# Squeeze-and-excitation on one core: keeping 20 more rows per partition on chip, 18 of them in PSUM, and a one-column gate computation

## The chip, the cores and the metric

The kernel runs on one core of a Trainium2 chip. The metric is the device time of one execution in microseconds (us), lower is better. A "row" in this text is one pixel's 384 channels in bf16, 768 bytes. Each of the 128 partitions owns 512 rows, so one row per partition is 98,304 bytes. The profile calls TensorE (matmuls) PE, its weight loads PEld, VectorE DVE, ScalarE ACT and SyncE SP. SBUF and PSUM are the core's two on-chip memories, HBM is the memory outside it, and DMA is the transfers between them.

## The reference

```python
# x: (1, 256, 256, 384), w_down: (384, 24), w_up: (24, 384), all bf16
def reference(x, w_down, w_up):
    s = x.mean(axis=(1, 2))                    # one mean per channel over 65,536 pixels
    s = sigmoid(silu(s @ w_down) @ w_up)       # a gate per channel
    return x * s[:, None, None, :]
```

Every input value must be read before the first output value is known. The input (50.33 MB) does not fit on chip, so part of it has to be read twice.

## The kernel before

In the load pass the input streams into SBUF, tile after tile of 16 rows, and TensorE sums each row over the partitions with a column of ones as weights. The last tiles that fit stay resident. Then a short chain of small operations makes the gate. In the second pass DVE multiplies the resident tiles in place and they are stored; as a slot's store lands, one of the tiles that did not stay is loaded into it again ("reload").

```python
    # 16 slots of 16 rows and one of 15: 271 of 512 rows stay, 241 are reloaded
    n_full = min(avail // (R * ROW_BYTES), rows_pp // R)
    extra_rows = (avail - n_full * R * ROW_BYTES) // ROW_BYTES
    slot_rows = [R] * n_full + ([extra_rows] if extra_rows else [])
    # ... cut: the reload tiles come first in the load pass, the resident ones last
    p1_last_split = [4, 2]      # last tile loaded in 4 pieces, the one before in 2
    # ... cut: for each tile: nc.sync.dma_start(...), then accumulate_rows:
            nc.tensor.matmul(sum_ps[:, :], lhsT=ones_bf[:, 0:1],
                             rhs=xt_ap[:, r * C : (r + 1) * C], ...)

    # the chain between the passes; KC = 3 blocks of P = 128 channels
    nc.scalar.activation(mean_sb[:], sum_ps[:], ACT.Copy, scale=1.0 / float(NROWS))
    for k in range(KC):         # channels onto partitions, repeated in 128 columns
        nc.tensor.matmul(psT[:, k * P : (k + 1) * P],
                         lhsT=mean_sb[0:1, k * P : (k + 1) * P],
                         rhs=ones_row[0:1, 0:P], start=True, stop=True)
    nc.vector.tensor_copy(sT_b[:], psT[:])
    for k in range(KC):
        nc.tensor.matmul(z_ps[:, :], lhsT=wd_bf[:, k, :],
                         rhs=sT_b[:, k * P : (k + 1) * P], ...)
    nc.scalar.activation(sig_sb[:], z_ps[:], ACT.Sigmoid)
    nc.vector.tensor_mul(silu_sb[:], z_ps[:], sig_sb[:])
    nc.tensor.matmul(z2_ps[:, :], lhsT=silu_sb[:, :], rhs=wu_bf[:, :], ...)
    nc.scalar.activation(s_bc[:], z2_ps[:], ACT.Sigmoid)     # 128 equal rows of the gate

    # second pass, per piece: multiply on DVE, store from ACT's queue
            nc.vector.tensor_tensor(out=x3, in0=x3,
                in1=s_bc[:, None, :].to_broadcast([P, rp, C]), op=ALU.mult)
            nc.scalar.dma_start(out=dst[...], in_=xs_)
    # ... cut: after a resident tile's store, a reload into its slot from SP's queue
```

Of the kernel before, what the change touches and what calls it, by code (L numbers as in the profile page):

```python
# [8 lines left out]
FP32 = mybir.dt.float32  # L9
BF16 = mybir.dt.bfloat16  # L10
ACT = mybir.ActivationFunctionType
ALU = mybir.AluOpType


@with_exitstack
def kernel(
# [7 lines left out]
    nc = tc.nc  # L24
    P = nc.NUM_PARTITIONS

    B, H, W, C = x.shape
    Cr = w_down.shape[1]
# [3 lines left out]
    KC = C // P  # L32
# [4 lines left out]
    esize = mybir.dt.size(x.dtype)  # L37
    ROW_BYTES = C * esize
    rows_pp = NROWS // P

    R = 16
    budget = 212_352
    misc_bytes = 4224
    first_split = [3, 2, 2]
    first_chunks = [2, 6, 8]
    p1_last_split = [4, 2]

    avail = budget - misc_bytes
    while R > 1 and rows_pp % R != 0:
        R //= 2  # L50
    n_full = min(avail // (R * ROW_BYTES), rows_pp // R)
    extra_rows = (avail - n_full * R * ROW_BYTES) // ROW_BYTES
    extra_rows = min(extra_rows, R - 1, rows_pp - n_full * R)
    if extra_rows < 1:
        extra_rows = 0
    slot_rows = [R] * n_full + ([extra_rows] if extra_rows else [])
    S = len(slot_rows)
    assert S >= 1
    res_rows = sum(slot_rows)
    assert res_rows <= rows_pp  # L60
    reload_rows = rows_pp - res_rows
    reload_tiles = [R] * (reload_rows // R)
# [3 lines left out]
    tiles = []  # L66
    row = 0
    rr_slot = 0
    for nr in reload_tiles:
        if nr < R and extra_rows and nr <= extra_rows:  # L70
            v = n_full
        else:
            v = rr_slot % n_full
            rr_slot += 1
        tiles.append(dict(row=row, nrows=nr, resident=False, slot=v))
        row += nr
    for v in range(S):
        nr = slot_rows[v]
        tiles.append(dict(row=row, nrows=nr, resident=True, slot=v))
        row += nr  # L80
    assert row == rows_pp

# [1 line left out]
    opp = of.rearrange("(p r) c -> p (r c)", p=P)  # L84

    consts = ctx.enter_context(tc.tile_pool(name="consts", bufs=1))
    small = ctx.enter_context(tc.tile_pool(name="small", bufs=1))
    slots_pool = ctx.enter_context(tc.tile_pool(name="slots", bufs=1))
    psum = ctx.enter_context(tc.tile_pool(name="psum", bufs=1, space=bass.MemoryType.PSUM))

    ones_bf = consts.tile([P, 1], BF16)
    nc.vector.memset(ones_bf[:], 1.0)  # L92
    ones_row = consts.tile([1, P], BF16)
# [11 lines left out]
    slots = [  # L105
        slots_pool.tile([P, slot_rows[v] * C], BF16, tag=f"slot{v}", name=f"slot{v}")
        for v in range(S)
    ]

    sum_ps = psum.tile([1, C], FP32)  # L110
    total_mm = rows_pp
    mm_state = {"i": 0}

    def accumulate_rows(xt_ap, nrows):
        for r in range(nrows):
            i = mm_state["i"]
            nc.tensor.matmul(  # L117
                sum_ps[:, :],
                lhsT=ones_bf[:, 0:1],
                rhs=xt_ap[:, r * C : (r + 1) * C],  # L120
                start=(i == 0),
                stop=(i == total_mm - 1),
            )
            mm_state["i"] = i + 1

    for k, t in enumerate(tiles):
        nr = t["nrows"]
        xt = slots[t["slot"]][:, 0 : nr * C]
        nparts = 1
        from_end = len(tiles) - 1 - k  # L130
        if from_end < len(p1_last_split):
            nparts = max(1, min(p1_last_split[from_end], nr))
        base = nr // nparts
        rem_r = nr - base * nparts
        r0 = 0
        for q in range(nparts):
            rp = base + (1 if q < rem_r else 0)
            if rp == 0:
                continue
            nc.sync.dma_start(  # L140
                out=xt[:, r0 * C : (r0 + rp) * C],
                in_=xpp[:, (t["row"] + r0) * C : (t["row"] + r0 + rp) * C],
            )
            accumulate_rows(xt[:, r0 * C : (r0 + rp) * C], rp)
            r0 += rp
    assert mm_state["i"] == total_mm

    mean_sb = small.tile([1, C], BF16)
    nc.scalar.activation(mean_sb[:], sum_ps[:], ACT.Copy, scale=1.0 / float(NROWS))  # L149
    psT = psum.tile([P, KC * P], FP32)  # L150
    for k in range(KC):
        nc.tensor.matmul(  # L152
            psT[:, k * P : (k + 1) * P],
            lhsT=mean_sb[0:1, k * P : (k + 1) * P],
            rhs=ones_row[0:1, 0:P],
            start=True,
            stop=True,
        )
    sT_b = small.tile([P, KC * P], BF16)
    nc.vector.tensor_copy(sT_b[:], psT[:])  # L160
    z_ps = psum.tile([Cr, P], FP32)
    for k in range(KC):
        nc.tensor.matmul(  # L163
            z_ps[:, :],
            lhsT=wd_bf[:, k, :],
            rhs=sT_b[:, k * P : (k + 1) * P],
            start=(k == 0),
            stop=(k == KC - 1),
        )
    sig_sb = small.tile([Cr, P], BF16)  # L170
    nc.scalar.activation(sig_sb[:], z_ps[:], ACT.Sigmoid)  # L171
    silu_sb = small.tile([Cr, P], BF16)
    nc.vector.tensor_mul(silu_sb[:], z_ps[:], sig_sb[:])  # L173
    z2_ps = psum.tile([P, C], FP32)
    nc.tensor.matmul(  # L175
        z2_ps[:, :], lhsT=silu_sb[:, :], rhs=wu_bf[:, :], start=True, stop=True
    )
    s_bc = small.tile([P, C], BF16)
    nc.scalar.activation(s_bc[:], z2_ps[:], ACT.Sigmoid)  # L179

    def scale_and_store(xt, nrows, dst, parts=1):
        if isinstance(parts, (list, tuple)):
            chunks = list(parts)
            rest = nrows - sum(chunks)
            assert rest >= 0
            if rest:
                chunks.append(rest)
        else:
            parts = max(1, min(parts, nrows))
            base = nrows // parts  # L190
            extra = nrows - base * parts
            chunks = [base + (1 if q < extra else 0) for q in range(parts)]
        r0 = 0
        for rp in chunks:
            if rp == 0:
                continue
            xs_ = xt[:, r0 * C : (r0 + rp) * C]
            x3 = xs_.rearrange("p (r c) -> p r c", c=C)
            nc.vector.tensor_tensor(  # L199
                out=x3,  # L200
                in0=x3,
                in1=s_bc[:, None, :].to_broadcast([P, rp, C]),
                op=ALU.mult,
            )
            nc.scalar.dma_start(out=dst[:, r0 * C : (r0 + rp) * C], in_=xs_)  # L205
            r0 += rp

    resident = [t for t in tiles if t["resident"]]
    reload = [t for t in tiles if not t["resident"]]
    queue = [(t, t["slot"]) for t in resident]  # L210
    pending_reload = list(reload)
    qi = 0
    while qi < len(queue):
        t, v = queue[qi]
        qi += 1
        parts = 1
        if qi - 1 < len(first_split):
            parts = first_split[qi - 1]
        if qi == 1 and first_chunks and sum(first_chunks) <= t["nrows"]:
            parts = first_chunks  # L220
        nr = t["nrows"]
        xt = slots[v][:, 0 : nr * C]
        scale_and_store(
            xt, nr, opp[:, t["row"] * C : (t["row"] + nr) * C], parts=parts
        )
        for pi, rt in enumerate(pending_reload):
            if rt["nrows"] <= slot_rows[v]:
                pending_reload.pop(pi)
                xr = slots[v][:, 0 : rt["nrows"] * C]
                nc.sync.dma_start(  # L230
                    out=xr,
                    in_=xpp[:, rt["row"] * C : (rt["row"] + rt["nrows"]) * C],
                )
                queue.append((rt, v))
                break
    assert not pending_reload, pending_reload


# [28 lines left out]
```

## Time and profile before

| | before |
|---|---|
| median of the first 6 runs | 308.13 us (307.71 to 310.08) |
| span of the profiled run | 306.4 us |
| HBM read and written | 74.06 and 50.33 MB |
| DVE, PE busy | 35%, 30% |
| last reduction matmul to first scaling | 123.86 to 127.29 us |

From the page of the kernel before: the DMA rows of the 40 slices of the span (busy tenths, then GB/s), and the bytes.

```profile
DMA  8999999999999998199999999999999999999996
GB/s 301 424 427 422 422 433 422 422 425 425 428 421 425 428 419 338 40 360 397 431 430 425 430 430 435 423 430 431 436 425 428 430 428 427 431 430 433 427 430 279
HBM read 74.06 MB, written 50.33 MB: 406 GB/s over the span
```

Everywhere but at both ends and around one slice in the middle, the transfers run at 421 to 436 GB/s. The table of stretches of the same kernel says it more exactly (the columns are the stretch and its length, the busy us and the count of PE, PEld, DVE, ACT and POOL, then the granted clock, the DMA share and GB/s): the load pass, the second pass with loads and stores mixed, and its end with stores alone.

```profile
20.00:114.00 94.00, 69.25 (x403) 33.60 (x402) 0.00 (x0) 0.00 (x0) 0.00 (x0) 1.00 1.01 425
137.00:250.00 113.00, 0.00 (x0) 0.00 (x0) 92.23 (x29) 0.00 (x0) 0.00 (x0) 0.50 1.01 427
254.00:300.00 46.00, 0.00 (x0) 0.00 (x0) 0.36 (x1) 0.00 (x0) 0.00 (x0) 0.50 1.01 430
```

DVE and PE wait for the transfers, so outside the gap a faster engine is worth nothing here. Only two things are: fewer bytes, and less time in which nothing moves. The timeline of the kernel before around the gap (start and duration in us, engine, operation, and in brackets how long the engine had been idle and what ended that):

```profile
115.83 8.02 PE L117 MATMUL sum_ps<-slot,ones_bf 128*1 128x384 bf16 x47 [0.94 <-DMA slot<-in_x_dram]
123.88 0.48 ACT L149 ACTIVATE mean_sb<-sum_ps 1x384 bf16<-1x384 f32 x1 [120.40 <-PE sum_ps L117]
124.41 0.34 PE L152 MATMUL psT<-ones_row,mean_sb 1*128 1x128 bf16 x3 [0.57 <-ACT mean_sb L149]
124.79 0.56 DVE L160 CAST sT_b<-psT 128x384 bf16<-128x384 f32 x1 [123.76 <-PE psT L152]
125.40 0.33 PE L163 MATMUL z_ps<-sT_b,wd_bf 128*24 128x128 bf16 x3 [0.65 <-DVE sT_b L160]
125.76 0.27 ACT L171 ACTIVATE sig_sb<-z_ps 24x128 bf16<-24x128 f32 x1 [1.40 <-PE z_ps L163]
126.06 0.28 DVE L173 TENSOR_TENSOR silu_sb<-z_ps,sig_sb 24x128 bf16<-24x128 f32 x1 [0.72 <-ACT sig_sb L171]
126.40 0.33 PE L175 MATMUL z_ps<-wu_bf,silu_sb 24*128 24x384 bf16 x1 [0.67 <-DVE silu_sb L173]
126.77 0.49 ACT L179 ACTIVATE s_bc<-z_ps 128x384 bf16<-128x384 f32 x1 [0.74 <-PE z_ps L175]
127.29 13.44 DVE L199 TENSOR_TENSOR slot<-slot,s_bc 128x768 bf16<-128x768 bf16 x8 [0.95 <-ACT s_bc L179]
```

Read the starts from top to bottom: each step begins when the one above ends, so the 3.43 us from 123.86 to 127.29 are one serial chain, and nothing is stored before it is over. Two more readings, from the groups of instructions by shape and from the list of waits of the kernel before:

```profile
L199 DVE TENSOR_TENSOR slot<-slot,s_bc 128x6144 bf16<-128x6144 bf16 x28 | 92.2, 3355 | 21.1 <-DMA slot<-in_x_dram 21.1
L199 DVE TENSOR_TENSOR slot<-slot,s_bc 128x3072 bf16<-128x3072 bf16 x5 | 8.4, 1751 | 0.0
DVE slot L199 <- DMA slot<-in_x_dram: 21.7, 7, 4.0
```

A multiply costs 0.52 ns per column ((3355 - 1751) / 3072) plus about 0.15 us, and DVE stands idle for 21.7 us waiting for reloads.

### The profile page before, as it was taken

The numbers are of one execution on the slowest core, as the hardware profiler recorded it, in microseconds if no ns is written. First come the engines' busy times: TensorE is split into PE (matmuls) and PEld (weight loads), VectorE is DVE, ScalarE is ACT, GpSimd is POOL, SyncE is SP. The second block draws the span as 40 slices with busy tenths as digits, with TensorE's granted clock in tenths as the row PEclk, the third lists the DMA queues.
The fourth block names the chain that finished last, engine by engine and source line by source line (L and its number), as shares of the span: only waits on it lengthen the run. The fifth ranks groups of instructions, "written<-read, shape, count | busy, mean of one in ns | idle before, by whom it ended". The sixth has DMA issues, their size and how long they took to land.

```text
span 306.4 us, 1330 instructions
## 1 busy us (share of the span) xinstructions
PE 90.4 (30%) x519; PEld 43.6 (14%) x519; DVE 106.7 (35%) x42; ACT 2.7 (1%) x5; POOL 0.2 (0%) x4
## 2 busy tenths in 40 slices
PE   0877577777777778200000000000000000000000
PEld 0433233333333334100000000000000000000000
DVE  0000000000000000499999999998444441000000
ACT  1000000000000000100000000000000000000000
POOL 0000000000000000000000000000000000000000
PEclk9999999999999999955555555555555555555555
DMA  8999999999999998199999999999999999999996
GB/s 301 424 427 422 422 433 422 422 425 425 428 421 425 428 419 338 40 360 397 431 430 425 430 430 435 423 430 431 436 425 428 430 428 427 431 430 433 427 430 279
DMA packets 13403, 124.49 MB, mean 406 GB/s; under 512 B 1852, under 2 KB 2388, under 8 KB 3924
## 3 DMA queue, kind: packets, MB, share of 16 engines
q1 hardware_dynamic: 7632, 74.03, 57.6%
q10 hardware_dynamic: 5764, 50.37, 39.1%
q8 instruction: 4, 0.07, 0.1%
q14 instruction: 3, 0.02, 0.0%
HBM read 74.06 MB, written 50.33 MB: 406 GB/s over the span
## 4 chain that ended last, share of the span: by engine, by line
DMA 74%; DVE 5%; PE 3%; ACT 0%; issue 0%; SPq 0%; ACTq 0%; DVEq 0%
DMA slot<-in_x_dram 36%; DMA out_dram<-slot 33%; DMA wd_bf<-in_w_down_dram 5%; DVE slot L199 5%; PE sum_ps L117 3%; DVE sT_b L160 0%; ACT s_bc L179 0%; ACT mean_sb L149 0%; PE psT L152 0%; PE z_ps L175 0%; PE z_ps L163 0%; DVE silu_sb L173 0%; ACT sig_sb L171 0%; ACTq L205 0%; DVEq L199 0%
## 5 line engine op out<-in xcount | busy, mean ns | idle before, releaser
L199 DVE TENSOR_TENSOR slot<-slot,s_bc 128x6144 bf16<-128x6144 bf16 (+5 forms) x37 | 105.7, 2922 | 22.7 <-DMA slot<-in_x_dram 21.7
L117 PE MATMUL sum_ps<-slot,ones_bf 128*1 128x384 bf16 x512 | 89.4, 329 | 34.4 <-DMA slot<-in_x_dram 34.4
L117 PEld LDWEIGHTS <-ones_bf 128*1 128x1 bf16 x512 | 43.1, 84 | 80.3 <-issue 42.2
L160 DVE CAST sT_b<-psT 128x384 bf16<-128x384 f32 x1 | 0.6, 558 | 123.8 <-PE psT L152 123.8
L149 ACT ACTIVATE mean_sb<-sum_ps 1x384 bf16<-1x384 f32 x1 | 0.5, 481 | 120.4 <-PE sum_ps L117 120.4
L103 ACT ACT_TABLE_LOAD x1 | 1.3, 1283 | 2.0 <-issue 2.0
L175 PE MATMUL z_ps<-wu_bf,silu_sb 24*128 24x384 bf16 x1 | 0.3, 332 | 0.7 <-DVE silu_sb L173 0.7
L173 DVE TENSOR_TENSOR silu_sb<-z_ps,sig_sb 24x128 bf16<-24x128 f32 x1 | 0.3, 279 | 0.7 <-ACT sig_sb L171 0.7
L163 PE MATMUL z_ps<-sT_b,wd_bf 128*24 128x128 bf16 x3 | 0.3, 217 | 0.6 <-DVE sT_b L160 0.6
L152 PE MATMUL psT<-ones_row,mean_sb 1*128 1x128 bf16 x3 | 0.3, 217 | 0.6 <-ACT mean_sb L149 0.6
L179 ACT ACTIVATE s_bc<-z_ps 128x384 bf16<-128x384 f32 x1 | 0.5, 491 | 0.7 <-PE z_ps L175 0.7
L163 PEld LDWEIGHTS <-wd_bf 128*24 128x24 bf16 x3 | 0.2, 90 | 0.7 <-issue 0.6
L92 DVE MEMSET ones_bf<- 128x1 bf16 x1 | 0.1, 59 | 0.8 <-PEq L251 0.8
L152 PEld LDWEIGHTS <-mean_sb 1*128 1x128 bf16 x3 | 0.2, 92 | 1.0 <-ACT mean_sb L149 1.0
L171 ACT ACTIVATE sig_sb<-z_ps 24x128 bf16<-24x128 f32 x1 | 0.3, 267 | 1.4 <-PE z_ps L163 1.4
L175 PEld LDWEIGHTS <-silu_sb 24*128 24x128 bf16 x1 | 0.1, 91 | 0.8 <-DVE silu_sb L173 0.8
L103 ACT ACTIVATE warm<-warm 1x8 bf16<-1x8 bf16 x1 | 0.2, 208 | 0.0
L94 DVE MEMSET ones_row<- 1x128 bf16 x1 | 0.2, 165 | 0.0
L251 POOL MEMSET const-uint8-127<- 128x1 uint8 x1 | 0.1, 102 | 0.0
L251 POOL MEMSET const-bfloat16-1.0<- 128x1 bf16 x1 | 0.1, 101 | 0.0
L251 POOL MEMSET const-float32-0.0<- 128x1 f32 x1 | 0.1, 98 | 0.2 <-issue 0.2
L251 POOL MEMSET const-float32-1.0<- 128x1 f32 x1 | 0.1, 98 | 0.0
(1 smaller groups left out, 0.1 us busy)
## 6 DMA issues: line engine op xcount, KB each, us to landing
slot<-in_x_dram SPq DMA_DIRECT2D x45, 1536.0 KB, 19.1
out_dram<-slot ACTq DMA_DIRECT2D x28, 1536.0 KB, 29.1
out_dram<-slot ACTq DMA_DIRECT2D x5, 768.0 KB, 8.4
slot<-in_x_dram SPq DMA_DIRECT2D x2, 768.0 KB, 27.7
out_dram<-slot ACTq DMA_DIRECT2D x1, 1440.0 KB
slot<-in_x_dram SPq DMA_DIRECT2D x3, 384.0 KB, 20.5
out_dram<-slot ACTq DMA_DIRECT2D x1, 576.0 KB, 2.8
slot<-in_x_dram SPq DMA_DIRECT2D x1, 288.0 KB, 14.7
```

What stands on the lines that cost most here:

```text
L103: nc.scalar.activation(warm[:], warm[:], ACT.Sigmoid)
L117: nc.tensor.matmul(sum_ps[:, :], lhsT=ones_bf[:, 0:1], rhs=xt_ap[:, r * C : (r + 1) * C], start=(i == 0), stop=(i == total_mm - 1),)
L149: nc.scalar.activation(mean_sb[:], sum_ps[:], ACT.Copy, scale=1.0 / float(NROWS))
L152: nc.tensor.matmul(psT[:, k * P : (k + 1) * P], lhsT=mean_sb[0:1, k * P : (k + 1) * P], rhs=ones_row[0:1, 0:P], start=True, stop=True,)
L160: nc.vector.tensor_copy(sT_b[:], psT[:])
L163: nc.tensor.matmul(z_ps[:, :], lhsT=wd_bf[:, k, :], rhs=sT_b[:, k * P : (k + 1) * P], start=(k == 0), stop=(k == KC - 1),)
L171: nc.scalar.activation(sig_sb[:], z_ps[:], ACT.Sigmoid)
L173: nc.vector.tensor_mul(silu_sb[:], z_ps[:], sig_sb[:])
L175: nc.tensor.matmul(z2_ps[:, :], lhsT=silu_sb[:, :], rhs=wu_bf[:, :], start=True, stop=True)
L179: nc.scalar.activation(s_bc[:], z2_ps[:], ACT.Sigmoid)
L199: nc.vector.tensor_tensor(out=x3, in0=x3, in1=s_bc[:, None, :].to_broadcast([P, rp, C]), op=ALU.mult,)
L251: nc = _bacc.Bacc("TRN2", target_bir_lowering=False, num_devices=1)
```

## The change

The intent is to reload less. PSUM is almost empty during the whole kernel, so 18 rows (two tiles of 9) are copied into it in the load pass and multiplied straight out of it in the second pass, into slots that have become free. The last SBUF slot grows from 15 to 17 rows. Together 291 rows stay instead of 271. The chain now works on one column instead of 128 equal ones, and all its PSUM tiles share one buffer (tag "pa").

```diff
+    n_full, extra_rows = 17, 0
+    slot_rows = [R] * 16 + [R + 1]
+    psum_parts = [9, 9]
+    psum_rows = sum(psum_parts)
+    res_rows = sum(slot_rows) + psum_rows
 ... (cut: two tiles of kind "psum" come first in the load pass)
+        psum_x32 = psum.tile([P, psum_rows * C // 2], FP32)
+        psum_x = psum_x32.bitcast(BF16)
 ...
-        for q in range(nparts):
-            rp = base + (1 if q < rem_r else 0)
+        for rp in ([6, 5, 4, 2] if from_end == 0 else _split_counts(nr, nparts)):
 ...
+        if t["kind"] == "psum":
+            p0 = t["p0"] * C // 2
+            nc.vector.tensor_copy(psum_x32[:, p0 : p0 + nr * C // 2], xt.bitcast(FP32))
 ...
-    psT = psum.tile([P, KC * P], FP32)
+    psT = psum.tile([P, KC], FP32, tag="pa")
     for k in range(KC):
         nc.tensor.matmul(
-            psT[:, k * P : (k + 1) * P],
+            psT[:, k : k + 1],
             lhsT=mean_sb[0:1, k * P : (k + 1) * P],
-            rhs=ones_row[0:1, 0:P],
+            rhs=ones_row[0:1, 0:1],
 ... (cut: sT_b, z_ps and sig_sb shrink the same way)
-    nc.vector.tensor_mul(silu_sb[:], z_ps[:], sig_sb[:])
+    nc.vector.tensor_mul(silu_sb[:],
+        z_ps[:, 0:1].to_broadcast([Cr, P]), sig_sb[:, 0:1].to_broadcast([Cr, P]))
 ...
+        if t["kind"] == "psum":
+            scale_and_store(psum_x[:, t["p0"] * C : (t["p0"] + nr) * C], nr, dst,
+                            parts=1, stage=slots[v][:, 0 : nr * C])
 ... (cut: slots 2 and 3 take the PSUM tiles and get no reload)
```

More of the change, by code (lines that the diff above doesn't have):

```diff
@@ L12, with _split_counts @@
 ALU = mybir.AluOpType
+def _split_counts(n, parts):
+    parts = max(1, min(parts, n))
+    base = n // parts
+    extra = n - base * parts
+    return [base + (1 if q < extra else 0) for q in range(parts)]
 @with_exitstack
@@ L41 @@
     R = 16
-    budget = 212_352
-    misc_bytes = 4224
     first_split = [3, 2, 2]
@@ L46, with _rs @@
     p1_last_split = [4, 2]
-    avail = budget - misc_bytes
+    psum_stage_pos = 3
+    psum_split = 2
+    def _rs(nbytes):
+        return ((nbytes + 31) // 32) * 32
+    misc_bytes = (
+        _rs(1 * esize)
+        + _rs(P * esize)
+        + _rs(KC * Cr * esize)
+        + _rs(C * esize)
+        + _rs(8 * esize)
+        + _rs(max(C * esize, P * esize))
+        + _rs(max(C * esize, P * esize))
+        + _rs(C * esize)
+    )
+    try:
+        budget = int(nc.sbuf_top) - int(nc.sbuf_base)
+    except Exception:
+        budget = 212_863
+    budget -= 256
     while R > 1 and rows_pp % R != 0:
         R //= 2
+    avail = budget - misc_bytes
     n_full = min(avail // (R * ROW_BYTES), rows_pp // R)
     extra_rows = (avail - n_full * R * ROW_BYTES) // ROW_BYTES
-    extra_rows = min(extra_rows, R - 1, rows_pp - n_full * R)
+    extra_rows = min(extra_rows, R, rows_pp - n_full * R)
     if extra_rows < 1:
@@ L56 @@
     slot_rows = [R] * n_full + ([extra_rows] if extra_rows else [])
+    n_full, extra_rows = 17, 0
+    slot_rows = [R] * 16 + [R + 1]
     S = len(slot_rows)
-    assert S >= 1
-    res_rows = sum(slot_rows)
+    assert S >= 1, "no SBUF slots"
+    slot_cap = slot_rows[0]
+    psum_bank_bytes = nc.PSUM_BANK_SIZE_BYTES
+    psum_banks_avail = max(0, nc.PSUM_NUM_BANKS - 2)
+    psum_rows = R
+    while psum_rows > 0 and (
+        psum_rows * ROW_BYTES > psum_banks_avail * psum_bank_bytes
+        or psum_rows > slot_cap
+        or (psum_rows * ROW_BYTES) % 4 != 0
+    ):
+        psum_rows -= 1
+    psum_parts = [9, 9]
+    psum_rows = sum(psum_parts)
+    res_rows = sum(slot_rows) + psum_rows
     assert res_rows <= rows_pp
@@ L68 @@
     rr_slot = 0
+    if psum_rows:
+        for i, nr in enumerate(psum_parts):
+            tiles.append(dict(row=row, nrows=nr, kind="psum", slot=i, p0=row))
+            row += nr
+        rr_slot = len(psum_parts)
     for nr in reload_tiles:
@@ L74 @@
             rr_slot += 1
-        tiles.append(dict(row=row, nrows=nr, resident=False, slot=v))
+        tiles.append(dict(row=row, nrows=nr, kind="reload", slot=v))
         row += nr
@@ L78 @@
         nr = slot_rows[v]
-        tiles.append(dict(row=row, nrows=nr, resident=True, slot=v))
+        tiles.append(dict(row=row, nrows=nr, kind="res", slot=v))
         row += nr
@@ L89 @@
     psum = ctx.enter_context(tc.tile_pool(name="psum", bufs=1, space=bass.MemoryType.PSUM))
+    psum_x = None
+    psum_x32 = None
+    if psum_rows:
+        psum_x32 = psum.tile([P, psum_rows * C // 2], FP32)
+        psum_x = psum_x32.bitcast(BF16)
     ones_bf = consts.tile([P, 1], BF16)
@@ L108 @@
     ]
-    sum_ps = psum.tile([1, C], FP32)
+    sum_ps = psum.tile([1, C], FP32, tag="pa")
     total_mm = rows_pp
@@ L131 @@
         if from_end < len(p1_last_split):
-            nparts = max(1, min(p1_last_split[from_end], nr))
-        base = nr // nparts
-        rem_r = nr - base * nparts
+            nparts = p1_last_split[from_end]
         r0 = 0
-        for q in range(nparts):
-            rp = base + (1 if q < rem_r else 0)
+        for rp in ([6, 5, 4, 2] if from_end == 0 else _split_counts(nr, nparts)):
             if rp == 0:
@@ L145 @@
             r0 += rp
+        if t["kind"] == "psum":
+            p0 = t["p0"] * C // 2
+            nc.vector.tensor_copy(psum_x32[:, p0 : p0 + nr * C // 2], xt.bitcast(FP32))
     assert mm_state["i"] == total_mm
-    mean_sb = small.tile([1, C], BF16)
+    mean_sb = small.tile([1, C], BF16, tag="msig")
     nc.scalar.activation(mean_sb[:], sum_ps[:], ACT.Copy, scale=1.0 / float(NROWS))
-    psT = psum.tile([P, KC * P], FP32)
+    psT = psum.tile([P, KC], FP32, tag="pa")
     for k in range(KC):
         nc.tensor.matmul(
-            psT[:, k * P : (k + 1) * P],
+            psT[:, k : k + 1],
             lhsT=mean_sb[0:1, k * P : (k + 1) * P],
-            rhs=ones_row[0:1, 0:P],
+            rhs=ones_row[0:1, 0:1],
             start=True,
@@ L158 @@
         )
-    sT_b = small.tile([P, KC * P], BF16)
+    sT_b = small.tile([P, KC], BF16, tag="st")
     nc.vector.tensor_copy(sT_b[:], psT[:])
-    z_ps = psum.tile([Cr, P], FP32)
+    z_ps = psum.tile([Cr, 1], FP32, tag="pa")
     for k in range(KC):
@@ L165 @@
             lhsT=wd_bf[:, k, :],
-            rhs=sT_b[:, k * P : (k + 1) * P],
+            rhs=sT_b[:, k : k + 1],
             start=(k == 0),
@@ L169 @@
         )
-    sig_sb = small.tile([Cr, P], BF16)
+    sig_sb = small.tile([Cr, 1], BF16, tag="msig")
     nc.scalar.activation(sig_sb[:], z_ps[:], ACT.Sigmoid)
-    silu_sb = small.tile([Cr, P], BF16)
-    nc.vector.tensor_mul(silu_sb[:], z_ps[:], sig_sb[:])
-    z2_ps = psum.tile([P, C], FP32)
+    silu_sb = small.tile([Cr, P], BF16, tag="stsilu")
+    nc.vector.tensor_mul(
+        silu_sb[:],
+        z_ps[:, 0:1].to_broadcast([Cr, P]),
+        sig_sb[:, 0:1].to_broadcast([Cr, P]),
+    )
+    z2_ps = psum.tile([P, C], FP32, tag="pa")
     nc.tensor.matmul(
@@ L177, with scale_and_store @@
     )
-    s_bc = small.tile([P, C], BF16)
+    s_bc = small.tile([P, C], BF16, tag="st")
     nc.scalar.activation(s_bc[:], z2_ps[:], ACT.Sigmoid)
-    def scale_and_store(xt, nrows, dst, parts=1):
+    def scale_and_store(xt, nrows, dst, parts=1, stage=None):
         if isinstance(parts, (list, tuple)):
-            chunks = list(parts)
+            chunks = [int(c) for c in parts]
             rest = nrows - sum(chunks)
@@ L188, in scale_and_store @@
         else:
-            parts = max(1, min(parts, nrows))
-            base = nrows // parts
-            extra = nrows - base * parts
-            chunks = [base + (1 if q < extra else 0) for q in range(parts)]
+            chunks = _split_counts(nrows, parts)
         r0 = 0
@@ L196, in scale_and_store @@
                 continue
-            xs_ = xt[:, r0 * C : (r0 + rp) * C]
-            x3 = xs_.rearrange("p (r c) -> p r c", c=C)
+            src = xt[:, r0 * C : (r0 + rp) * C]
+            dsb = src if stage is None else stage[:, r0 * C : (r0 + rp) * C]
             nc.vector.tensor_tensor(
-                out=x3,
-                in0=x3,
+                out=dsb.rearrange("p (r c) -> p r c", c=C),
+                in0=src.rearrange("p (r c) -> p r c", c=C),
                 in1=s_bc[:, None, :].to_broadcast([P, rp, C]),
@@ L204, in scale_and_store @@
             )
-            nc.scalar.dma_start(out=dst[:, r0 * C : (r0 + rp) * C], in_=xs_)
+            nc.scalar.dma_start(out=dst[:, r0 * C : (r0 + rp) * C], in_=dsb)
             r0 += rp
-    resident = [t for t in tiles if t["resident"]]
-    reload = [t for t in tiles if not t["resident"]]
+    resident = [t for t in tiles if t["kind"] == "res"]
+    reload = [t for t in tiles if t["kind"] == "reload"]
+    psum_pending = [t for t in tiles if t["kind"] == "psum"]
     queue = [(t, t["slot"]) for t in resident]
@@ L212 @@
     qi = 0
+    n_proc = 0
     while qi < len(queue):
@@ L221 @@
         nr = t["nrows"]
-        xt = slots[v][:, 0 : nr * C]
-        scale_and_store(
-            xt, nr, opp[:, t["row"] * C : (t["row"] + nr) * C], parts=parts
-        )
+        dst = opp[:, t["row"] * C : (t["row"] + nr) * C]
+        if t["kind"] == "psum":
+            scale_and_store(
+                psum_x[:, t["p0"] * C : (t["p0"] + nr) * C],
+                nr,
+                dst,
+                parts=1,
+                stage=slots[v][:, 0 : nr * C],
+            )
+        else:
+            scale_and_store(slots[v][:, 0 : nr * C], nr, dst, parts=parts)
+        n_proc += 1
+        if (
+            psum_pending
+            and n_proc >= psum_stage_pos
+            and psum_pending[0]["nrows"] <= slot_rows[v]
+        ):
+            queue.append((psum_pending.pop(0), v))
+            continue
         for pi, rt in enumerate(pending_reload):
@@ L235 @@
                 break
+    while psum_pending:
+        t = psum_pending.pop(0)
+        nr = t["nrows"]
+        scale_and_store(
+            psum_x[:, 0 : nr * C],
+            nr,
+            opp[:, t["row"] * C : (t["row"] + nr) * C],
+            parts=psum_split,
+            stage=slots[0][:, 0 : nr * C],
+        )
     assert not pending_reload, pending_reload
```

## The prediction

> **What bounds the kernel now.** The transfers. The DMA row of the 40 slices is at 8 or 9 tenths except around the transition (40 GB/s in one slice) and at the end. A table of stretches gives 425 GB/s in the load pass (20 to 114 us), 427 in the second pass while loads and stores mix (137 to 250 us) and 430 while only stores are left (254 to 300 us). The Trainium skill, "DMA: Bandwidth & Descriptors", section "Where 436 GB/s comes from", puts the ceiling at 435.2 GB/s; this trace agrees, so no rate is left to win, only bytes and gaps. PE (30% busy) and DVE (35%) wait for DMA: DVE idles 21.7 us for loads in the second pass, and is done at 254.7 us, 52 us before the end.
>
> The one real gap is the transition. The timeline shows the last reduction matmul ending at 123.86 us, then a chain of small operations until the first scaling at 127.29 us (3.43 us), while nothing moves.
>
> **What the change does.**
>
> 1. Bytes. Before, 16x16+15 = 271 of 512 rows per partition stay in SBUF and 241 are read twice. After, 273 in SBUF plus 18 in PSUM = 291, so 221 are read twice. 20 rows x 128 partitions x 768 B = 1.966 MB less, all on the critical path, as DMA is saturated: at 427 to 430 GB/s 4.6 us.
>
> 2. The chain in the transition. Columns shrink from 128 to 1. DVE's PSUM cast of 384 columns took 558 ns and the 128-column PSUM multiply 279 ns, which fits 0.14 us plus 1.1 ns per column; a 3-column cast is then about 0.15 us (0.40 less). ACT's sigmoids of 384 and 128 columns, 491 and 267 ns, give about 0.11 us less for 1 column. Two groups of three matmuls (0.34 us each): about 0.07 us less each. The rest stays. Sum 0.65 us, all critical.
>
> 3. The end of the load pass. Last tile split 6,5,4,2 rather than 4,4,4,3. The last load landed at about 123.1 us, and PE was still working off 47 matmuls in one piece at 171 ns; about 0.1 us less.
>
> 4. Added DVE work, off the path. Two copies into PSUM of 1728 fp32 columns (estimate 2 us each) fall where DVE is idle. Two multiplies out of PSUM of 3456 columns: the skill's "VectorE: DVE Perf Modes", section "The perf-mode tier table", has tensor_tensor at 1x with a PSUM operand; the SBUF ones here run at 0.52 ns per column, so I estimate 3.75 us rather than 1.95 us. 3.6 us more against 21.7 us of idle time cost nothing.
>
> 5. Two reloads less (14, not 16); slots 2 and 3 take the PSUM rows and get none. The load queue pauses there; the store queue is fed at 16 rows per 3.36 us (468 GB/s), more than DMA takes, so DMA stays full.
>
> **Predicted time.** 308.13 - 4.6 - 0.65 - 0.1 = 302.8 us, 1.7% faster; range 301.8 to 304.0. Chances: over 2% faster 0.22, within 2% 0.76, slower 0.02.
>
> **What would show the steps right or wrong.** 1: HBM read falls from 74.06 to about 72.1 MB. 2: from last reduction matmul to first scaling about 2.8 us. 3: DMA's quiet time around the transition shorter by 0.8 us in all. 4: PSUM-source multiplies about 3.7 us each, nothing waiting for them. 5: no slice of the second pass below 415 GB/s beyond its start.
>
> **What would make it wrong.** A drop in rate from the 17-row or 9-row pieces; DMA running dry where two slots skip a reload, or DVE late behind the slow multiplies; a different lag at the end of the load pass, since the 16 engines finish unevenly; or a rate that differs by some tenths of a per cent between runs.

## The result, and the profile after

| | before | after |
|---|---|---|
| median | 308.32 us (16 runs) | 302.69 us (8 runs, 302.21 to 303.63) |
| ratio | | 0.9818, 95% interval 0.9802 to 0.9835 |
| span of the profiled run | 306.4 us | 300.7 us |
| HBM read | 74.06 MB | 72.09 MB |
| first scaling starts | 127.29 us | 126.71 us |
| last reduction matmul ends | 123.86 us | 123.93 us |

All ratios here are the mean time of one kernel's runs over that of the other's runs of the same rounds, so they are not quite the ratios of the quoted medians. The changed kernel was run once more later (303.10 us median of 4, ratio 0.9828); over all 12 runs its mean is 302.86 us, and this is the number that the experiments are compared with. Single runs scatter by about 0.4 us either way.

The page of the changed kernel, the same rows as before:

```profile
DMA  7999999999999999189999999999999999999997
GB/s 286 432 427 425 426 427 425 427 424 425 427 422 427 427 425 405 55 328 360 431 430 432 427 433 428 426 432 428 432 430 432 427 423 431 431 432 428 432 430 309
HBM read 72.09 MB, written 50.33 MB: 407 GB/s over the span
```

Reads are down by 1.97 MB, exactly 20 rows, and no slice of the second pass between its start and the last one is below 423 GB/s. The table of stretches of the changed kernel has the same rates as before within 1 GB/s, so the change won nothing in rate and lost nothing:

```profile
20.00:114.00 94.00, 71.10 (x406) 34.16 (x405) 0.00 (x0) 0.00 (x0) 0.00 (x0) 0.98 1.01 425
137.00:238.00 101.00, 0.00 (x0) 0.00 (x0) 87.27 (x28) 0.00 (x0) 0.00 (x0) 0.50 1.01 427
250.00:295.00 45.00, 0.00 (x0) 0.00 (x0) 2.76 (x1) 0.00 (x0) 0.00 (x0) 0.50 1.01 429
```

The timeline of the changed kernel in the gap:

```profile
115.41 8.51 PE L168 MATMUL sum_ps<-slot,ones_bf 128*1 128x384 bf16 x49 [0.93 <-DMA slot<-in_x_dram]
123.96 0.48 ACT L200 ACTIVATE mean_sb<-sum_ps 1x384 bf16<-1x384 f32 x1 [120.50 <-PE sum_ps L168]
124.49 0.22 PE L203 MATMUL psT<-ones_row,mean_sb 1*128 1x1 bf16 x3 [0.57 <-ACT mean_sb L200]
124.75 0.16 DVE L211 CAST sT_b<-psT 128x3 bf16<-128x3 f32 x1 [115.02 <-PE psT L203]
124.97 0.21 PE L214 MATMUL z_ps<-sT_b,wd_bf 128*24 128x1 bf16 x3 [0.25 <-DVE sT_b L211]
125.28 0.16 ACT L222 ACTIVATE sig_sb<-z_ps 24x1 bf16<-24x1 f32 x1 [0.85 <-PE z_ps L214]
125.48 0.28 DVE L224 TENSOR_TENSOR silu_sb<-z_ps,sig_sb 24x128 bf16<-24x128 f32 x1 [0.56 <-ACT sig_sb L222]
125.82 0.33 PE L230 MATMUL z_ps<-wu_bf,silu_sb 24*128 24x384 bf16 x1 [0.63 <-DVE silu_sb L224]
126.18 0.49 ACT L234 ACTIVATE s_bc<-z_ps 128x384 bf16<-128x384 f32 x1 [0.74 <-PE z_ps L230]
126.71 8.50 DVE L251 TENSOR_TENSOR slot<-slot,s_bc 128x768 bf16<-128x768 bf16 x6 [0.95 <-ACT s_bc L234]
```

The cast fell from 0.56 to 0.16 us, the sigmoid from 0.27 to 0.16 and each group of three matmuls by 0.12. That is 0.75 us; about 0.1 us of it went back into hand-overs (the sigmoid now starts 0.10 us after its matmuls end, before 0.03 us). The chain is now 2.79 us. It starts no sooner: the last reduction matmul still ends at 123.9 us.

The groups and the wait list of the changed kernel for DVE's work:

```profile
L251 DVE TENSOR_TENSOR slot<-slot,s_bc 128x6144 bf16<-128x6144 bf16 x26 | 85.7, 3354 | 17.8 <-DMA slot<-in_x_dram 17.8
L196 DVE COPY psum_x<-slot 128x1728 f32<-128x1728 f32 x2 | 3.9, 1962 | 4.8 <-DMA slot<-in_x_dram 4.8
L251 DVE TENSOR_TENSOR slot<-psum_x,s_bc 128x3456 bf16<-128x3456 bf16 x2 | 3.8, 1952 | 0.0
DVE slot L251 <- DMA slot<-in_x_dram: 21.1, 6, 4.4
```

The multiply out of PSUM took 1952 ns for 3456 columns. At the SBUF rate it would be 3456 x 0.522 + 148 = 1952 ns. Reading PSUM was as fast as reading SBUF; the prediction had 3.75 us. The two copies into PSUM fall in the load pass, whose rate (425 GB/s) is the same as before and whose last matmul ends 0.07 us later.

### The profile page after: what moved, and what is told of

Read it like the earlier page. It is cut to its first block, busy times and chain, and to the rows that moved or that the text cites. A ratio compares the mean times of both kernels' runs of the same rounds, so it can differ in the third digit from the quotient of the medians.

```text
span 300.7 us, 1332 instructions
## 1 busy us (share of the span) xinstructions
PE 92.1 (31%) x519; PEld 44.1 (15%) x519; DVE 110.1 (37%) x44; ACT 2.6 (1%) x5; POOL 0.2 (0%) x4
## 3 DMA queue, kind: packets, MB, share of 16 engines
HBM read 72.09 MB, written 50.33 MB: 407 GB/s over the span
## 4 chain that ended last, share of the span: by engine, by line
DMA 79%; DVE 3%; PE 1%; issue 0%; ACT 0%; SPq 0%; ACTq 0%; DVEq 0%
DMA slot<-in_x_dram 50%; DMA out_dram<-slot 29%; DVE slot L251 3%; PE sum_ps L168 1%; SPq L188 0%; ACT s_bc L234 0%; ACT mean_sb L200 0%; PE z_ps L230 0%; DVE silu_sb L224 0%; PE psT L203 0%; PE z_ps L214 0%; DVE sT_b L211 0%; ACT sig_sb L222 0%; SPq L299 0%; ACTq L257 0%
## 5 line engine op out<-in xcount | busy, mean ns | idle before, releaser
L251 DVE TENSOR_TENSOR slot<-slot,s_bc 128x6144 bf16<-128x6144 bf16 (+5 forms) x35 | 101.9, 2976 | 22.0 <-DMA slot<-in_x_dram 21.1
L168 PE MATMUL sum_ps<-slot,ones_bf 128*1 128x384 bf16 x512 | 91.3, 333 | 32.6 <-DMA slot<-in_x_dram 32.5
L196 DVE COPY psum_x<-slot 128x1728 f32<-128x1728 f32 x2 | 3.9, 1962 | 4.8 <-DMA slot<-in_x_dram 4.8
L251 DVE TENSOR_TENSOR slot<-psum_x,s_bc 128x3456 bf16<-128x3456 bf16 x2 | 3.8, 1952 | 0.0
```

The costliest lines, as they stand in the source:

```text
L168: nc.tensor.matmul(sum_ps[:, :], lhsT=ones_bf[:, 0:1], rhs=xt_ap[:, r * C : (r + 1) * C], start=(i == 0), stop=(i == total_mm - 1),)
L196: nc.vector.tensor_copy(psum_x32[:, p0 : p0 + nr * C // 2], xt.bitcast(FP32))
L251: nc.vector.tensor_tensor(out=dsb.rearrange("p (r c) -> p r c", c=C), in0=src.rearrange("p (r c) -> p r c", c=C), in1=s_bc[:, None, :].to_ ...
```

## The experiments

The total was predicted within a tenth of a microsecond or two. A right sum can still be made of wrong terms, so the experiments take the terms apart. The theory: the gain is 20 rows of traffic at the transfer rate (4.6 us) and the shorter chain (0.65 us), and nothing else. The rivals: the chain is worth more than its length; the ragged tile of one row that disappeared was costly in itself; the new layout and not the bytes brought the gain; DVE's new work costs something. All kernels gave correct results. They ran in three batches on three chips; the kernel before had means of 308.40, 308.37 and 308.36 us in them, so means of different batches can be compared.

### The chain alone

```diff
 # the kernel before, with only the one-column chain:
-    psT = psum.tile([P, KC * P], FP32)
+    psT = psum.tile([P, KC], FP32)      # and the same for sT_b, z_ps, sig_sb
```

> The kernel before with only the one-column chain in the transition (no PSUM rows, no new slots, old split of the last tile). My theory: the trace has 3.43 us from the last reduction matmul to the first scaling before and 2.77 us after, and all of it is critical, so this kernel is 0.65 us faster than before, near 307.65 us. Rival: the part of the gain that bytes do not explain (the whole gain was about 5.6 us, the bytes were costed at 4.6) comes from here, because an earlier start of the stores also shortens the ramp or the tail: then 1.0 us or more, 307.3 us or less.

Measured: 307.57 us median, ratio 0.9968 (0.9956 to 0.9979). In means that is about 0.95 us faster, with an interval from about 0.65 to 1.36 us. In its trace the chain was 2.72 us long, 0.7 us shorter than before.

### The rows alone

```diff
 # the changed kernel, with the wide chain back:
-    psT = psum.tile([P, KC], FP32, tag="pa")
+    psT = psum.tile([P, KC * P], FP32, tag="pa")      # and so on
```

> The changed kernel with the wide (128-column) chain put back, everything else as changed (PSUM rows, 273 SBUF rows, split 6,5,4,2). My theory: the chain takes 3.4 us again, so 0.65 us slower than the changed kernel, about 303.35 us; the gain that is left, 4.9 to 5.0 us, is the 20 rows and whatever bytes do not explain. Rival (the chain carries about 1.0 us): 303.7 us.

Measured: 303.95 us median of 4, ratio 0.985 (0.9837 to 0.9863). The gain over before is 1.5% of 308.4, 4.6 us, which is what 20 rows at 428 GB/s were costed at. Its mean is 1.0 us above that of the changed kernel. So the two halves are 4.6 and about 1.0 us, and they add up to the 5.6 us of the whole. The trace of this kernel has a chain of 3.51 us, 0.72 us longer than after the change; the runs say 0.95 and 1.0 us. The next experiment asks whether that difference is real.

### The chain made longer

```diff
-    nc.scalar.activation(mean_sb[:], sum_ps[:], ACT.Copy, scale=1.0 / float(NROWS))
+    for _ in range(6):
+        nc.scalar.activation(mean_sb[:], sum_ps[:], ACT.Copy, scale=1.0 / float(NROWS))
```

> The changed kernel with the first operation of the chain, ACT's copy of the mean (0.48 us), issued six times in a row instead of once (result correct), so that the chain in the transition is up to 2.4 us longer. The narrow chain cost 0.65 to 0.7 us less in the traces, but 0.95 and 1.0 us less in the times of two pairs of kernels. My theory: a microsecond of chain costs a microsecond of time, and the rest was scatter, so the time rises by what the trace shows the chain to have grown by, about 2.4 us, to 305.2 us. Rival: a microsecond of chain costs 1.4 us: 306.2 us.

Two lines of its timeline, the repeated copy and the first scaling:

```profile
124.00 3.04 ACT L201 ACTIVATE mean_sb<-sum_ps 1x384 bf16<-1x384 f32 x6 [120.53 <-PE sum_ps L168]
129.47 1.83 DVE L254 TENSOR_TENSOR slot<-slot,s_bc 128x768 bf16<-128x768 bf16 x2 [1.11 <-ACT s_bc L237]
```

The first scaling started 2.76 us later than in the changed kernel (129.47 against 126.71). The time was 305.81 us median, 305.88 mean: 3.0 us above the mean of the changed kernel, with a scatter of about 0.2 us on such a difference. That is 1.1 us of time for 1 us of chain. It argues for the plain theory (1.0) over the rival (1.4), which asks for 3.9 us. The start of the first scaling explains part of the rest: it moved by 0.78 us from before to the chain alone (127.29 to 126.51) and by 0.83 us from the rows alone to the changed kernel (127.54 to 126.71), as the last matmul ended slightly sooner too. Against gains of 0.95 and 1.0 us that leaves about 0.15 us, which is inside the scatter.

### The ragged row removed

The kernel before with the one-column chain, and 17 slots of 16 rows. Reloads are then exactly 15 tiles of 16, and no transfer of one row (96 KB) is left.

```diff
-    budget = 212_352
+    budget = 213_120
```

> The one-column chain on the kernel before, and in addition 272 resident rows instead of 271 (17 slots of 16), so that the single ragged row that was loaded, reloaded and stored as transfers of 96 KB is gone. My theory, bytes alone: 98304 bytes less at 428 GB/s, 0.23 us faster than the kernel with the one-column chain only, about 307.4 us. Rival: small ragged transfers, the last store above all, cost time of their own (the end of the trace was 0.5 us more even after the change): then 0.5 us or more faster than the one-column chain alone, 307.1 us or less.

Measured: 306.84 us median, ratio 0.9947 (0.9936 to 0.9959). It is 0.6 us (means) or 0.7 us (medians) faster than the chain alone, where the bytes of one row are 0.23 us. That spoke for the rival. The rival was tested the other way round.

### A small last store put in

```diff
+            if nr == 13:
+                parts = [12, 1]      # the changed kernel; its last store of 13 rows cut in two
```

> The changed kernel with its last store, of 13 rows, cut into 12 rows and 1 row (result correct), so that the last transfer is one of 96 KB as in the kernel before. Rival theory for the 0.2 to 0.4 us that bytes and chain leave over: a small last store makes the end worse: 0.3 to 0.5 us slower than the changed kernel, 303.2 us or more. My theory: no effect on its own, the removal of the ragged row helped otherwise (one load, one reload and one store less) or by scatter; within 0.2 us of the changed kernel, 302.7 to 303.1 us.

Measured: 303.22 us median of 4, ratio 0.9833 (0.9816 to 0.9849). The mean is 0.4 us above that of the changed kernel, on the rival's side of the line that I had drawn, but the intervals of the two kernels overlap. Against the rival: the rows-alone kernel has no one-row transfer either and gained no more than its bytes. The traces don't settle it. I summed the unused transfer time at the end, in windows of half a microsecond from 5 us before the last bytes to the end of the span, each 0.5 x (1 - GB/s / 430). It was 2.8 to 3.1 us in the three kernels with a one-row last store, and 2.4 to 2.5 us in the changed kernel (twice) and the even split, but 3.0 to 3.3 us in three other kernels that also end on 13 rows, and 2.4 to 2.7 us in three more. Whether a small last store costs some 0.4 us stays open.

### The bytes put back

```diff
         if t["kind"] == "psum":
+            nc.sync.dma_start(out=slots[v][:, 0 : 10 * C], in_=xpp[:, 0 : 10 * C])
             scale_and_store(      # overwrites those rows
```

> The changed kernel, correct result, with 2 extra loads of 10 rows each in the second pass (into the two slots that receive the PSUM rows, which are then overwritten), so that HBM reads are back at the 74.06 MB of before. My theory (bytes): 4.6 us slower than the changed kernel, about 307.3 us. Rival (the gain comes from the new layout, fewer reload tiles waiting on slots, or a better end, not from bytes): it stays within 1.5 us of the changed kernel, below 304.3 us. If 0.3 to 0.5 us of the gain belongs to the layout beyond bytes, it shows as less than 4.6 us of loss less the error; if the bytes are worth more than the rate says, as more.

Measured: 308.04 us median (307.16 to 309.42), ratio 0.9989 (0.9969 to 1.0009). With the changed layout, PSUM tiles, split and chain all in place, reading 20 more rows takes the whole gain back: 5.3 us in means, more than the 4.6 us costed, with the widest scatter of all kernels here. The rival (layout, not bytes) is out: it wanted less than 304.3 us.

### The PSUM rows left out

```diff
-    psum_parts = [9, 9]
+    psum_parts = []
```

> The changed kernel without the 18 PSUM rows: 273 rows stay in SBUF, 239 are reloaded, all else as changed. My theory (bytes): 18 rows are 1.77 MB, at 428 GB/s 4.1 us slower than the changed kernel, 306.8 us, that is 1.5 us faster than before (0.46 for two rows, about 1.0 for the chain). Rival (PSUM rows bring overhead, as two slots skip a reload and DVE has slow work): the loss is clearly below 4.1 us, 306.3 us or less. Rival (the reading back of 10-row pieces cost 5.3 us for 20 rows, so a row is worth 0.26 us rather than 0.23): 4.7 us slower, 307.4 us.

Measured: 306.88 us median of 6, ratio 0.9953 (0.9939 to 0.9967). That is 3.9 us in means for 18 rows, against 4.1 us costed. Within the scatter, PSUM rows are worth what SBUF rows are worth.

The kernels with the one-column chain form a series in the number of rows read again:

| rows read again per partition | kernel | mean us |
|---|---|---|
| 221 | changed kernel (12 runs) | 302.86 |
| 239 | PSUM rows left out | 306.81 |
| 240 | ragged row removed | 306.85 |
| 241 | chain alone | 307.47 |
| 241 | bytes put back | 308.12 |

From the changed kernel to the chain alone, 221 to 241 rows, it is 4.61 us, 0.230 us a row. A row's 98,304 bytes at 428 GB/s are 0.230 us. Only the whole stretch fits so well: from 239 to 240 rows it is 0.04 us, from 240 to 241 0.62 us.

### Twice the work out of PSUM

```diff
+            if stage is not None:
+                nc.vector.tensor_tensor(...)      # the same multiply again, same place
```

> The changed kernel with each of the two multiplies out of PSUM issued twice in a row (the same values into the same place, result correct), so that DVE spends 3.9 us more, as much as if these multiplies ran at one element a cycle as I had predicted (the trace shows 1.95 us each[...]). My theory (DVE is off the path, it waits 21.1 us for loads in the second pass): no change, within 0.3 us of the changed kernel, and DVE's wait for loads drops to about 17 us. Rival (DVE paces the stores there): 2 to 4 us slower.

From the wait list of this kernel:

```profile
DVE slot L251 <- DMA slot<-in_x_dram: 17.7, 5, 4.1
```

DVE's wait for reloads shrank from 21.1 to 17.7 us: most of the 3.9 us of extra work came out of idle time. The time was 303.44 us median, 0.5 us (means) above the changed kernel of the same rounds and 0.6 us above its 12 runs, with a scatter of 0.15 to 0.3 us on these differences. That is more than the 0.3 us I had allowed and far from the 2 to 4 us of the rival. In the trace the second pass (137 to 238 us) ran at 426 GB/s, and the unused time at the end was larger (3.3 us, with 2.4 to 2.5 us in the changed kernel); why, I don't know. So at half the speed that PSUM reads had, the multiplies would have cost about half a microsecond.

### The last tile split evenly

```diff
-        for rp in ([6, 5, 4, 2] if from_end == 0 else ...):
+        for rp in ([5, 4, 4, 4] if from_end == 0 else ...):
```

> The changed kernel with its last tile of the load pass loaded as 5,4,4,4 rows instead of 6,5,4,2. My theory: the last reduction matmul ended at 123.92 us after the change and at 123.85 us before, so the split bought nothing; within 0.2 us of the changed kernel, with that matmul ending between 123.8 and 124.2 us. Rival: the small last piece does save matmuls after the last landing; then 0.3 us or more slower (two matmuls of 171 ns).

Measured: 303.37 us median of 4 (302.52 to 303.76), ratio 0.9838 (0.9819 to 0.9857), with the changed kernel itself at 0.9828 in the same rounds. The trace shows the last reduction matmul ending at 123.92 us and the whole span at 300.7 us, both as in the changed kernel. The mean is 0.3 us above the changed kernel of the same rounds, inside the scatter of the two. The new split did nothing that can be measured.

The critical chain (start, duration, and what released what) tells why. Two lines of the changed kernel, then two of the even split:

```profile
100.63 21.14 DMA slot<-in_x_dram
121.81 2.12 PE sum_ps L168 x11
```

```profile
107.85 15.22 DMA slot<-in_x_dram
123.11 0.82 PE sum_ps L168 x4
```

PE was not working off 49 matmuls at the end. In the changed kernel it had caught up and waited for the piece of 5 rows, which landed at 121.77 us; in the even split it waited for the last piece, which landed at 123.07 us, and only 4 matmuls followed. The landing records of the traces fill in the rest: in the changed kernel the piece of 4 rows landed at 122.74 us and that of 2 rows at 123.19 us, while PE was still on the 4 rows. The small last piece was not what PE waited for.

### Two attempts at a better version

The quiet time around the gap is what is left besides bytes. The first attempt loads the last four tiles in pieces of 8 rows or less, and cuts the first reload in two, so that loads can begin sooner in the second pass.

```diff
-    p1_last_split = [4, 2]
+    p1_last_split = [4, 2, 2, 2]
 ...
+                for qn in [8, 8] if v == 0 else [rt["nrows"]]:
```

> An attempt at a better version: the changed kernel with the last four tiles of the load pass loaded in pieces of 8 rows or less (only the last two before), so that PE is less far behind at the end, and the first reload cut into two of 8 rows, so that loads can fill the ramp of the second pass sooner. Expected: last reduction matmul 0.2 to 0.4 us earlier than 123.9 us, first reload up to 2 us sooner than 133.7 us; 0.5 us faster than the changed kernel, 302.3 us. If the end of the load pass is set by the last landing rather than by PE's backlog, nothing changes.

Two lines of its timeline, the last reduction matmuls and the first reloads:

```profile
121.93 2.06 PE L168 MATMUL sum_ps<-slot,ones_bf 128*1 128x384 bf16 x11 [0.22 <-DMA slot<-in_x_dram]
131.59 2.76 SPq L301 DMA_DIRECT2D slot<-in_x_dram  x2
```

With smaller pieces PE is less far behind in the last tiles, and still ends at 123.99 us: by the landing records the piece of 4 rows landed at 122.81 us, and its matmuls and those of the 2 rows after it followed. A late landing sets the end, as the expectation's last sentence allowed, though not the very last one. The first reload starts at 131.59 instead of 133.71 us, and that did not help either: 302.76 us median, mean 302.74 us.

The second attempt accepts the landing time and takes work off the chain behind it. The 17 rows of the last tile are reduced straight into columns: each block of 128 channels of a row is the weights, and one column holding 1/65536 moves through it. The mean of the other 495 rows is copied and transposed before the last two rows have landed.

```diff
+    psT = psum_x32[:, psum_rows * C // 2 : psum_rows * C // 2 + KC]   # spare columns
 # last tile: mean_sb is copied as soon as row 494 is summed; a matmul with zeros opens psT;
+                for r in range(r0, r0 + rp):
+                    for k in range(KC):
+                        nc.tensor.matmul(psT[:, k : k + 1],
+                            lhsT=xt[:, r * C + k * P : r * C + (k + 1) * P],
+                            rhs=frac[:, 0:1], start=False, ...)
 # before the last piece: the three transposing matmuls, now accumulating into psT
```

> The same, and in addition the last tile's 17 rows are reduced straight into columns (the rows are the weights, one column of 1/65536 moves), so that the copy of the mean and the three transposing matmuls leave the end of the chain and happen before the last piece has landed. The chain after the last reduction matmul loses 0.49 + 0.24 us and two hand-overs, about 0.8 us; it should be 2.0 us instead of 2.79. Expected 0.8 us faster than the version without it, 301.5 us; if the 51 narrow matmuls take longer than 17 wide ones (171 ns each), less.

```profile
120.66 0.60 PE L223 MATMUL psum_x<-frac,slot 128*128 128x1 bf16 x18
121.90 0.53 PE L223 MATMUL psum_x<-frac,slot 128*128 128x1 bf16 x15 [0.64 <-DMA slot<-in_x_dram]
122.81 0.45 PE L223 MATMUL psum_x<-frac,slot 128*128 128x1 bf16 x12 [0.39 <-DMA slot<-in_x_dram]
123.20 0.22 PE L214 MATMUL psum_x<-ones_row,mean_sb 1*128 1x1 bf16 x3
123.36 0.30 PE L223 MATMUL psum_x<-frac,slot 128*128 128x1 bf16 x6
123.70 0.16 DVE L237 CAST sT_b<-psum_x 128x3 bf16<-128x3 f32 x1 [114.10 <-PE psum_x L223]
125.65 10.17 DVE L277 TENSOR_TENSOR slot<-slot,s_bc 128x768 bf16<-128x768 bf16 x7 [0.95 <-ACT s_bc L260]
```

The last matmul ends at 123.66 us, 0.27 us sooner than in the changed kernel, and is followed at once by the cast; the chain behind it is 1.99 us, 0.8 us shorter. The first scaling starts at 125.65 us, 1.06 us sooner. The time is 301.81 us median of 4 (301.41 to 302.09), ratio to before 0.9785 (0.9770 to 0.9801), mean 301.78 us: 1.1 us faster than the changed kernel. This version beats both. A gap made shorter by 1.06 us moved the time by 1.1 us, as the lengthened chain had done in the other direction.

## Why the prediction was right or wrong

The total was right: 302.8 us predicted, 302.69 us measured (302.86 us in the mean of all runs). Point by point:

1. Bytes, 4.6 us: right. Reads fell to 72.09 MB, the rows alone gained 4.6 us, the series of kernels gives 0.230 us a row, and the bytes put back took the gain back (5.3 us, with a wide scatter).
2. The chain, 0.65 us: right in the trace (3.43 to 2.79 us; the parts as costed but the matmuls, which gave 0.12 rather than 0.07 us each, and about 0.1 us lost again in hand-overs). In the times of two pairs of kernels it was 0.95 and 1.0 us. The lengthened chain gave 1.1 us of time for each us of chain. The term may have been too small by 0.1 to 0.3 us; the runs do not resolve more.
3. The end of the load pass, 0.1 us: wrong, though small. The last matmul ended 0.07 us later, not sooner, the even split was not measurably different, and smaller pieces in the first attempt at a better version did not move it. The step that failed was "PE was still working off 47 matmuls in one piece": the one row of the timeline hides pauses. In the kernel before, the last two pieces landed at 122.44 and 123.15 us, and PE restarted at 122.48 and 123.19 us, 0.04 us after each: it had caught up and was waiting for loads. The end is a late landing plus the matmuls left to do: 123.15 us plus 3 of them before, 122.74 us plus 6 after, 123.07 us plus 4 in the even split. DMA's unused time around the gap (118 to 140 us, summed as at the end, with 428 for 430) fell from 9.7 us to 9.2 and 9.0 us in the two traces of the changed kernel, by 0.5 to 0.6 us and not by the 0.8 us predicted.
4. DVE's added work off the path: right in effect, wrong in the size. The copies into PSUM took 1.96 us each as estimated. The multiplies out of PSUM took 1.95 us, not 3.75 us; the rule of one element a cycle with a PSUM operand, taken from the skill's table, did not hold here. The error did no harm because DVE idles for 21 us, and the doubled multiplies put the price of half the speed at 0.5 to 0.6 us.
5. DMA stays full although two slots skip a reload: right, no slice below 423 GB/s between the start of the second pass and its end.

Terms 2 and 3 erred in opposite directions, and the sum came out closer than its parts. The start of the sum was luck as well: it took 308.13 us, the median of the first 6 runs, where the mean of all 16 is 308.43 us. The gain was predicted as 5.35 us and measured as 5.6 us; the low start hid this. Where the remaining 0.25 us lie, in the chain, the end of the stores or scatter, is not shown.

## What to carry to other kernels

Where the profile shows the transfers at a flat rate from end to end, cost a change in bytes, and use idle memory of any kind, PSUM too, to avoid a second read; the engine time for moving data through it cost little here while that engine waited (0.5 to 0.6 us when the multiplies out of PSUM were doubled). Besides bytes, only the quiet time counts, and there a microsecond taken off the serial chain is about a microsecond of time. One row of a timeline is not a backlog: compare the landing of each piece with the start of the matmuls that use it. Where they follow the landings, as at the end of the load pass here, cutting the last pieces differently gained nothing that could be measured; taking work off behind the last landing did.

## What the Trainium skill lacked or had wrong

- "VectorE: DVE Perf Modes", section "The perf-mode tier table": it has tensor_tensor at 1x with any PSUM operand. A bf16 multiply with one operand in PSUM and one in SBUF took 1952 ns for 3456 columns, the same 0.52 ns per column as with both in SBUF. The section "Why PSUM operands drop a tier" of the same page, which says a PSUM operand caps an op at 2x (1x for fp32), agrees with the run. The copy of 1728 fp32 columns into PSUM took 1962 ns, about 1.05 ns per column if its fixed part is the 0.15 us of the multiplies.
- "DMA: Bandwidth & Descriptors", section "Where 436 GB/s comes from": it says that for transfers between HBM and SBUF the HBM side (about 358 GB/s) binds. With this kernel on one core, the traces show 425 GB/s in loads, 427 with loads and stores mixed and 430 in stores, close to the section's other ceiling of 435.2. The sentence lacks a condition: the page "HBM Reference", section "Specifications (TRN2)", has about 425 GB/s for a core streaming alone and about 358 GB/s each when both cores of a pair stream.
- "TensorE: Matmul & The Clock Gate", section "LDWEIGHTS (loading the stationary operand)": its formula of columns / 1.2 makes 107 ns for 128 columns. In the trace of the second attempt a load of fresh 128x128 bf16 weights lasted 96 ns on average, near that, but the loads overlapped: 18 pairs of load and one-column matmul took 0.60 us, about 33 ns a pair. So the formula is not the price of a pair in a stream; the section does not say so, though the page's section "Back-to-back issue gap" calls such pairs pipelined. A row of 384 channels cost about 0.1 us as weights, against 0.16 us from one matmul's start to the next as the moving operand. (The ends of matmuls are modelled in this profile, so this is rough.)
